# MLP products of two x tiles ahead of the projections, and adds moved from VectorE to DMA

## Chip, cores and metric

The kernel runs on one core of a Trainium2 chip. The metric is device time in microseconds of one execution; lower is better. Engines are called as the profile calls them: PE (TensorE), PEld (its weight loads), DVE (VectorE), ACT (ScalarE), POOL (GpSimd) and SP (SyncE). SP, ACT and POOL each also issue DMA transfers on a queue of their own.

## What is computed

Two branches on one input x (2048 rows of 512, bf16) are mixed by a gate per row. Cut to what matters:

```python
g = sigmoid((x * gate_w).sum(-1))
# A: 32 heads of 16; each row attends to 8 rows, 2 apart, behind it
q, k, v = split(x @ wqkv)
logits = einsum("bhsd,bhswd->bhsw", q, k[pos - 2*w]) * 16 ** -0.5     # w = 0..7
attn = softmax(where(pos - 2*w >= 0, logits, -1e9))
a = einsum("bhsw,bhswd->bhsd", attn, v[pos - 2*w]) @ wo
# B: an MLP over the rows, after a layer norm over the 512 columns
u = gelu(einsum("bsd,sf->bdf", layernorm(x), w1) + b1)                # F = 1792
b = transpose(einsum("bdf,fs->bds", u, w2) + b2)
out = g * a + (1 - g) * b
```

The inputs A_x and B_x have the same shape; both branches of the kernel read A_x.

## The kernel before

The program records every operation of every engine in a list with its reads and writes. A planner (`_Sched`) gives each operation an expected duration, runs a list schedule over five engines and so writes out the order on each engine; `plan_waits` then turns what is left of the dependences into semaphore waits. Each engine executes its list strictly in order. PE's main operations (`PE(...)`) are chained in the order of the program; only a few, such as the head-dim sums, are placed by the planner among them. The lists are emitted inside an `nc.Block()`, one function per engine (L890 to L908).

**Projections.** x is needed transposed (XT). The first 512 rows are transposed on PE (L548) and copied out by DVE and ACT (`ext`, L559); the other three groups of 512 rows come by transposing DMAs on SP's queue (L476). `f_q0` (L569) computes the first 512 rows of Q in two halves with 256-column matmuls, and `f_proj` (L613) everything else: K, Q and V, each in four head-dim groups `dl` and four row groups `sb`, four matmuls of 512 columns each. ACT copies each result from its PSUM bank (line L443 is the helper of all ACT operations). The banks rotate over seven, for V over three.

**Layer norm.** DVE computes statistics of the 16 x tiles (L652), some tiny operations give mean and deviation of all tiles at once (ACT: Ln and Exp), and 16 operations (L666) normalise X in place.

**Attention.** DVE does the work (L440 is the helper of all its two-input operations). The rows are handled in two halves h. For each half: four products `qk` of a Q group with eight shifted views of a K group, 8192 elements per partition each (two halves of 4096 in h = 0), two adds `qa` that join pairs of them, into buffers P0 to P2. Then `f_sum` (L683) on PE sums over the head-dim that lies across partitions, with a 0/1 matrix, reading both of the remaining buffers and accumulating them in PSUM banks 4 to 7; in h = 0 it also computes the gate's dot products (L677). ACT copies the logits out (`lev`), DVE and ACT do the softmax (`mx`, `msub`, `exp`, `sm`, `lns`, `rsz`, `rb`, `nrm`), and 16 DMAs per half on POOL's queue (L735) spread the weights over partitions. Then come the weighted values in eight units of 256 rows: a product `avm` of 8192 elements per partition, and adds of 4096 (`ava`), 2048 (`avb`) and 1024 (`avc`), the last into OT. Even units use buffer P1 and odd ones P0.

**MLP.** `f_ph2` (L769): 14 tiles of F, each 16 matmuls over the x tiles, W1 in three rotating slots, GELU on ACT. `f_ph3` (L795): 16 output tiles of rows, each 14 matmuls (the last tile in two column halves), with W2 in slots that reuse the memory of finished tensors. The attention's output product `f_wo` (L804, 4 matmuls) adds into the same bank, five tiles behind the MLP product; ACT scales and shifts the result by the gate (`ev`) and SP stores it. Unit u of the attention serves output tiles 2u and 2u + 1, so the last tiles wait for the last sum of unit 7.

Of the kernel before, what the change touches and what calls it, by code (L numbers as in the profile page):

```python
# [12 lines left out]
S = 2048  # L13
D = 512
# [13 lines left out]
NOELIDE = False  # L28

# [40 lines left out]
class _Sched:  # L70
# [72 lines left out]
    def _pass(self, ops, extra, dma_bw, dma_lat):  # L143
# [20 lines left out]
        dma_free = 0.0  # L164
# [8 lines left out]
        while nleft:  # L173
# [21 lines left out]
            if op.is_dma:  # L195
                clock[e] = st + op.dur
                xs = max(st + 0.3, dma_free)
                xd = max(op.nbytes / dma_bw, 0.05)
                dma_free = xs + xd
                op.end = max(dma_free, clock[e]) + dma_lat  # L200
            else:
                op.end = st + op.dur
                clock[e] = op.end
# [98 lines left out]
def bass_gated_mix__sliding_local_dilated__mixer_token_mlp__prompt_kernel(nc, A_x, A_wqkv, A_wo, B_x, B_w1, B_b1, B_w2, B_b2, gate_w, out, dbg=None):  # L302
    with contextlib.ExitStack() as es:
        block = es.enter_context(nc.Block())
# [56 lines left out]
        XTALL = ["xt0_%d_%d" % (hb, d0) for hb in range(2) for d0 in (0, 2)] + ["xt1", "xt2", "xt3"]  # L361
# [5 lines left out]
        PR = [["p0"], ["p1"], ["p2", "p2h"]]  # L367
# [4 lines left out]
        PB = [view("P%d" % b, BF16, [(HS, NW), (1, HS)]) for b in range(3)]  # L372
# [45 lines left out]
        NMR = small(NST)  # L418
        E1 = small(NST)
# [77 lines left out]
        ld_wq("wq0", 0, 2, "wq0")  # L497
        ld_wq("wq1", 2, 4, "wq1")
        ld_x(0, 1)
        ld_x(1, 1)  # L500
        ld_x(2, 2)
        ld_w("wk", 1, 0, 4, "wk")
        ld_xt(1)
# [10 lines left out]
        def ld_w1(j):  # L514
            load("w1_%d" % j, W1W[:, j % 3, :, :], w1v[:, :, 256 * j:256 * j + 256], S * 256 * 2, ["w1s%d" % (j % 3)], order=j < 3)
# [10 lines left out]
        def f_warm(n):  # L526
            def fn(e):
                ins = None
                for _ in range(n):
                    ins = e.matmul(ps[:, 7, :], lhsT=ONES, rhs=ONES4, start=True, stop=True)  # L530
                return ins
            return fn
# [8 lines left out]
        PE(f_warm(5), 2.1, ["ones"], ["b7"], "warm")  # L541

        def f_tx(t):
            def fn(e):
                ins = None
                for dt in range(4):
                    o_ = (dt % 2) * 256 + (t % 2) * 128
                    ins = e.transpose(out=psb(4 + 2 * (t // 2) + dt // 2)[:, o_:o_ + 128],  # L548
                                      in_=X[:, t, dt * 128:(dt + 1) * 128], identity=IDENT)
                return ins  # L550
            return fn

        def xt_ev(hb):
            for eng, d0 in (("dve", 0), ("act", 2)):
                bk = 4 + 2 * hb + d0 // 2
                src = psb(bk)[:, 0:512]
                dst = sub(XT, d0 * S + hb * 256, [(S, 2), (1, 256)])
                if eng == "dve":
                    A("dve", (lambda s_, d_: lambda e: e.tensor_copy(out=d_, in_=s_))(src, dst), 0.4, reads=["b%d" % bk],  # L559
                      writes=["xt0_%d_%d" % (hb, d0)], name="ext%d_%d" % (hb, d0))  # L560
                else:
                    A("act", act(dst, src, AF.Copy), 0.6, reads=["b%d" % bk],
                      writes=["xt0_%d_%d" % (hb, d0)], name="ext%d_%d" % (hb, d0))

        def f_q0(hb, dt):
            def fn(e):
                ins = None
                for dl in range(4):
                    ins = e.matmul(ps[:, dl, hb * 256:hb * 256 + 256], lhsT=sub(WQKV, dt * 3 * D + dl, [(4, 128)]),  # L569
                                   rhs=XT[:, dt, hb * 256:hb * 256 + 256], start=(dt == 0), stop=(dt == 3))  # L570
                return ins
            return fn

        for hb in range(2):
            for t in (2 * hb, 2 * hb + 1):
                PE(f_tx(t), 0.35, ["x%d" % t, "ident"], ["b%d" % (4 + 2 * hb), "b%d" % (5 + 2 * hb)], "tx%d" % t)
            xt_ev(hb)
            for dt in range(4):
                PE(f_q0(hb, dt), 0.44, ["xt0_%d_%d" % (hb, 2 * (dt // 2)), "wq%d" % (dt // 2)], ["b%d" % dl for dl in range(4)], "q0_%d_%d" % (hb, dt))
        XT0 = ["xt0_%d_%d" % (hb, d0) for hb in range(2) for d0 in (0, 2)]  # L580
# [18 lines left out]
        for dl in range(4):  # L599
            evac(0, dl, 0, dl)  # L600

        ring = [0, [4, 5, 6, 7, 0, 1, 2]]
# [15 lines left out]
        WR = {0: ["wq0", "wq1"], 1: ["wk"], 2: ["wv"]}  # L618
# [6 lines left out]
        def f_tb(e):  # L625
            e.transpose(out=psb(3)[:, 0:NFT], in_=B1R, identity=IDENT[0:NFT, 0:NFT])
            e.transpose(out=psb(3)[:, 64:68], in_=GWR, identity=IDENT[0:4, 0:4])
            return e.transpose(out=psb(3)[:, 32:32 + NST], in_=B2R, identity=IDENT[0:NST, 0:NST])

        for dl in range(4):  # L630
            proj(1, dl, 0)
        PE(f_tb, 0.3, ["b1r", "b2r", "gwr", "ident"], ["b3"], "t_b12")
        A("dve", lambda e: e.tensor_copy(out=GWREP, in_=sub(psb(3), 64, [(1, 4), (0, 32)])), 0.2, reads=["b3"], writes=["gwrep"], name="gwrep", prio=-20)
        A("dve", lambda e: e.tensor_copy(out=B1C, in_=psb(3)[:, 0:NFT]), 0.15, reads=["b3"], writes=["b1c"], name="b1c", prio=-20)
        A("dve", lambda e: e.tensor_copy(out=B2C, in_=psb(3)[:, 32:32 + NST]), 0.15, reads=["b3"], writes=["b2c"], name="b2c", prio=-20)
        for dl in range(4):
            proj(0, dl, 1)
            proj(1, dl, 1)
# [6 lines left out]
        ring[0], ring[1] = 0, [0, 1, 2]  # L645
        for dl in range(4):
            for sb in range(4):
                proj(2, dl, sb)


        for t in range(NST):
            A("dve", (lambda t_: lambda e: e.bn_stats(out=ST6[:, t_, :], in_=X[:, t_, :]))(t), 0.67,  # L652
              reads=["x%d" % t], writes=["st%d" % t], name="st%d" % t, prio=-20)
        STS = ["st%d" % t for t in range(NST)]
# [3 lines left out]
        A("dve", tt(MD, MD, MD, ALU.mult), 0.12, reads=[], writes=["md"], name="ln_md2", prio=-20)  # L658
        A("dve", lambda e: e.scalar_tensor_tensor(out=VV, in0=MD, scalar=128.0, in1=VV, op0=ALU.mult, op1=ALU.add), 0.12,
          reads=["md"], writes=["vv"], name="ln_var", prio=-20)  # L660
        A("act", act(SD, VV, AF.Ln, bias=1e-5, scale=1.0 / 512), 0.25, reads=["vv"], writes=["sd"], name="ln_log", prio=-20)
        A("act", act(RSTD, SD, AF.Exp, scale=-0.5), 0.25, reads=["sd"], writes=["rstd"], name="ln_rstd", prio=-20)
        A("dve", lambda e: e.scalar_tensor_tensor(out=NMR, in0=MS, scalar=-0.5, in1=RSTD, op0=ALU.mult, op1=ALU.mult), 0.15,
          reads=["ms", "rstd"], writes=["nmr"], name="ln_nmr", prio=-20)
        for t in range(NST):
            A("dve", (lambda t_: lambda e: e.tensor_scalar(out=X[:, t_, :], in0=X[:, t_, :], scalar1=col(RSTD, t_), scalar2=col(NMR, t_),  # L666
                                                           op0=ALU.mult, op1=ALU.add))(t), 0.33,
              reads=["rstd", "nmr", "st%d" % t], writes=["x%d" % t], name="ln%d" % t, prio=-10)


        def f_sum(h, b0, b1, with_gate):
            def fn(e):
                ins = None
                if with_gate:
                    for dt in range(4):
                        for c in range(4):
                            ins = e.matmul(ps[32 * c:32 * c + 32, 3, :], lhsT=GWREP[:, dt, :],  # L677
                                           rhs=sub(XT, dt * S + c * UT_, [(HS, 2), (1, UT_)]),
                                           start=(dt == 0), stop=(dt == 3), tile_position=(0, 32 * c))
                for wp in range(4):  # L680
                    for k_, b_ in enumerate((b0, b1)):
                        for c in range(4):
                            ins = e.matmul(ps[32 * c:32 * c + 32, 4 + wp, :], lhsT=RP,  # L683
                                           rhs=sub(PB[b_], 2 * wp * HS + c * UT_, [(HS, 2), (1, UT_)]),
                                           start=(k_ == 0), stop=(k_ == 1), tile_position=(0, 32 * c))
# [4 lines left out]
        PLAN = {0: ((0, 1), (1, 2)), 1: ((2, 0), (0, 1))}  # L690
        for h in range(2):
            for pr in range(2):
                bb = PLAN[h][pr]
                for k_ in range(2):
                    dl = 2 * pr + k_
                    for s_, n_ in (((0, 512), (512, 512)) if h == 0 else ((0, HS),)):
                        sbs = [2 * h + x_ for x_ in range(s_ // 512, (s_ + n_) // 512)]
                        A("dve", tt(sub(PB[bb[k_]], s_, [(HS, NW), (1, n_)]), sub(QH[h], dl * HS + s_, [(0, NW), (1, n_)]),
# [238 lines left out]
```

## Time and profile before

| | |
|---|---|
| time, median of 3 runs | 172.63 us (171.09 to 173.3) |
| profiled execution, first to last instruction (its span) | 170.8 us |
| around the span (172.63 less 170.83) | 1.8 us, if the profiled execution was like the median one |
| PE busy | 164.1 us |
| DVE busy | 152.3 us, of which 134.7 in L440 |
| ACT busy | 79.4 us |
| POOL busy | 19.5 us, 16.3 of it issuing the 32 DMAs of L735 |
| last sum on DVE ends | 166.2 us |
| PE ends | 168.2 us |

The page of the profile gives the busy time of each engine, the chain of work that ended last (followed backwards from the last instruction to what released it), and groups of instructions with their busy time, mean time of one, and idle time ahead. Further answers of the trace give the instructions in order of time. Lines of the form "start, us, engine line op xcount [idle before <- who ended it]" are such an answer; matmuls overlap in the pipeline, so a group's total is divided by its count, and the mean of a single one is longer than the distance to the next.

### The profile page before, as it was taken

The numbers are of one execution on the slowest core, as the hardware profiler recorded it, in microseconds if no ns is written. First come the engines' busy times: TensorE is split into PE (matmuls) and PEld (weight loads), VectorE is DVE, ScalarE is ACT, GpSimd is POOL, SyncE is SP. The second block draws the span as 40 slices with busy tenths as digits, with TensorE's granted clock in tenths as the row PEclk, the third lists the DMA queues.
The fourth block names the chain that finished last, engine by engine and source line by source line (L and its number), as shares of the span: only waits on it lengthen the run. The fifth ranks groups of instructions, "written<-read, shape, count | busy, mean of one in ns | idle before, by whom it ended". The sixth has DMA issues, their size and how long they took to land.

```text
span 170.8 us, 2097 instructions
## 1 busy us (share of the span) xinstructions
PE 164.1 (96%) x846; PEld 79.8 (47%) x846; DVE 152.3 (89%) x115; ACT 79.4 (46%) x107; POOL 19.5 (11%) x57
## 2 busy tenths in 40 slices
PE   6889999999999999999999998999999999999983
PEld 2574555555554444444443443444444444444732
DVE  2516998999999989999998998999999999999981
ACT  3119677666665189987424697000022211111172
POOL 7000000000000000000198001970000000000000
PEclk9999999999999999999999999999999999999999
DMA  5999999800000095987599999998000010100023
GB/s 165 273 240 267 300 300 290 256 1 2 4 0 0 26 308 135 285 210 209 160 240 230 360 301 283 308 351 285 7 31 31 31 35 31 60 32 31 31 74 110
DMA packets 43128, 26.87 MB, mean 157 GB/s; under 512 B 7536, under 2 KB 41968, under 8 KB 43120
## 3 DMA queue, kind: packets, MB, share of 16 engines
q1 hardware_dynamic: 40800, 21.96, 47.9%
q0 software_dynamic: 1632, 4.21, 7.9%
q10 hardware_dynamic: 688, 0.59, 1.1%
q8 instruction: 6, 0.10, 0.2%
q14 instruction: 2, 0.02, 0.0%
HBM read 18.88 MB, written 2.10 MB: 123 GB/s over the span
## 4 chain that ended last, share of the span: by engine, by line
DVE 51%; PE 33%; ACT 6%; DMA 4%; issue 3%; POOL 1%; SPq 0%; DVEq 0%
DVE arena L440 50%; PE ps L613 22%; PE ps L769 4%; ACT arena L443 4%; PE ps L569 3%; ACT L872 2%; DMA arena<-arena 2%; DMA arena<-in_A_x_dram 2%; PE ps L804 1%; PE ps L683 1%; POOL arena L735 1%; PE ps L677 1%; PE ps L548 1%; DVE arena L559 0%; DVE arena L652 0%
## 5 line engine op out<-in xcount | busy, mean ns | idle before, releaser
L440 DVE TENSOR_TENSOR arena<-arena 128x2048 bf16<-128x2048 bf16 (+10 forms) x72 | 134.7, 1902 | 3.5 <-PE ps L683 1.0
L795 PE MATMUL ps<-arena 128*128 128x512 bf16 (+1 forms) x238 | 50.3, 367 | 0.7 <-ACT arena L443 0.7
L443 ACT ACTIVATE arena<-ps,arena 128x512 bf16<-128x512 f32 (+1 forms) x30 | 21.5, 727 | 60.9 <-PE ps L804 49.8
L769 PE MATMUL ps<-arena 128*128 128x512 bf16 x224 | 49.0, 379 | 0.0
L443 ACT ACTIVATE arena<-ps 128x512 bf16<-128x512 f32 (+3 forms) x53 | 33.4, 649 | 23.7 <-PE ps L613 10.4
L613 PE MATMUL ps<-arena 128*128 128x512 bf16 x176 | 38.3, 379 | 0.0
L795 PEld LDWEIGHTS ps<-arena 128*128 128x128 bf16 x238 | 23.2, 98 | 26.2 <-ACT arena L443 1.2
L769 PEld LDWEIGHTS ps<-arena 128*128 128x128 bf16 x224 | 21.7, 98 | 26.6 <-issue 0.8
L613 PEld LDWEIGHTS ps<-arena 128*128 128x128 bf16 x176 | 19.8, 113 | 17.7
L735 POOL DMA_DIRECT2D arena<-arena x32 | 16.3, 515 | 93.8 <-DVE arena L440 93.8
L872 ACT ACT_TABLE_LOAD x14 | 18.0, 1283 | 2.1 <-issue 1.8
L804 PE MATMUL ps<-arena 128*128 128x512 bf16 (+1 forms) x68 | 15.8, 367 | 0.7 <-DVE arena L440 0.7
L652 DVE BATCH_NORM_STATS2 arena<-arena 128x6 f32<-128x512 bf16 x16 | 10.1, 681 | 4.3 <-DMA arena<-in_A_x_dram 4.3
L804 PEld LDWEIGHTS ps<-arena 128*128 128x128 bf16 x68 | 6.6, 98 | 8.1 <-DVE arena L440 1.2
L443 ACT ACTIVATE arena<-arena 128x16 f32<-128x16 f32 (+5 forms) x10 | 6.8, 679 | 2.5 <-DVE arena L440 2.4
L569 PE MATMUL ps<-arena 128*128 128x256 bf16 x32 | 5.5, 346 | 1.0 <-DVE arena L559 1.0
L666 DVE TENSOR_SCALAR arena<-arena 128x512 bf16<-128x512 bf16 x16 | 5.3, 405 | 0.0
L569 PEld LDWEIGHTS ps<-arena 128*128 128x128 bf16 x32 | 3.9, 129 | 2.5 <-DVE arena L559 1.6
L683 PE MATMUL ps<-arena 128*32 128x512 bf16 x64 | 3.8, 380 | 0.0
L559 DVE COPY arena<-ps 128x512 bf16<-128x512 bf16 x2 | 0.8, 425 | 3.0 <-PE ps L548 3.0
L530 PE MATMUL ps<-arena 128*128 128x512 bf16 x5 | 2.3, 629 | 1.1 <-POOL arena L446 1.1
L548 PE MATMUL ps<-arena 128*128 128x128 bf16 x16 | 2.3, 308 | 0.6 <-DMA arena<-in_A_x_dram 0.6
(34 smaller groups left out, 13.0 us busy)
## 6 DMA issues: line engine op xcount, KB each, us to landing
arena<-in_B_w_dram SPq DMA_DIRECT2D x7, 1024.0 KB, 8.1
arena<-in_B_w_dram SPq DMA_DIRECT2D x8, 896.0 KB, 8.6
arena<-arena POOLq DMA_DIRECT2D x32, 128.0 KB, 7.3
out_dram<-arena SPq DMA_DIRECT2D x15, 128.0 KB, 1.7
arena<-in_A_x_dram SPq DMA_DIRECT2D x3, 512.0 KB, 4.3
arena<-in_A_wqkv_dram SPq DMA_DIRECT2D x2, 512.0 KB, 6.0
arena<-in_A_wqkv_dram ACTq DMA_DIRECT2D x2, 256.0 KB, 3.6
arena<-in_A_wo_dram SPq DMA_DIRECT2D x1, 512.0 KB, 8.7
```

The costliest lines, as they stand in the source:

```text
L440: return lambda e: e.tensor_tensor(out=o_, in0=a_, in1=b_, op=op_)
L443: return lambda e: e.activation(out=o_, in_=i_, func=f_, **kw)
L569: ins = e.matmul(ps[:, dl, hb * 256:hb * 256 + 256], lhsT=sub(WQKV, dt * 3 * D + dl, [(4, 128)]), rhs=XT[:, dt, hb * 256:hb * 256 + 256], ...
L613: ins = e.matmul(ps[:, bank, :], lhsT=sub(WQKV, dt * 3 * D + tn * D + dl, [(4, 128)]), rhs=XT[:, dt, sb * 512:(sb + 1) * 512], start=(dt = ...
L652: A("dve", (lambda t_: lambda e: e.bn_stats(out=ST6[:, t_, :], in_=X[:, t_, :]))(t), 0.67, reads=["x%d" % t], writes=["st%d" % t], name="s ...
L666: A("dve", (lambda t_: lambda e: e.tensor_scalar(out=X[:, t_, :], in0=X[:, t_, :], scalar1=col(RSTD, t_), scalar2=col(NMR, t_), op0=ALU.mu ...
L683: ins = e.matmul(ps[32 * c:32 * c + 32, 4 + wp, :], lhsT=RP, rhs=sub(PB[b_], 2 * wp * HS + c * UT_, [(HS, 2), (1, UT_)]), start=(k_ == 0), ...
L735: prev = sch.dma("pool", (lambda d_, s_: lambda e: e.dma_start(d_, s_))(dst, src), 131072, ds, issue=1.0, reads=["att%d" % h], writes=["av ...
L769: ins = e.matmul(ps[:, bank, :], lhsT=W1W[:, (ft // 2) % 3, st, 128 * (ft % 2):128 * (ft % 2) + 128], rhs=X[:, st, :], start=(st == 0), st ...
L795: ins = e.matmul(ps[:, bank, 0:c1 - c0], lhsT=W2S[i // 2][:, ft, 128 * (i % 2):128 * (i % 2) + 128], rhs=UT[:, ft, c0:c1], start=(ft == 0) ...
L804: ins = e.matmul(ps[:, bank, 0:c1 - c0], lhsT=OT[:, i // 2, dl, 128 * (i % 2):128 * (i % 2) + 128], rhs=WO[:, dl, c0:c1], start=False, sto ...
L872: e.preload_act_table_set(want)
```

## The change

- **Lead.** Two x tiles are normalised alone and at once: their own statistics, aggregate (`bn_aggr`), Ln, Exp and scaling. `f_lead` then does the matmuls of these tiles for the first GL = 4 tiles of F, into banks 0 to 3, before any projection. The partial sums stay there until the MLP's own time, when these four F tiles begin at x tile 2. The parts of W1 that this needs (`ld_strip`) come on ACT's queue at the start; the loads of W1 slots 0 and 1 leave them out. Around the transposes stand 8 filler matmuls on constants instead of 5.
- **Start.** x tiles 2 and 3 are loaded separately; Wq is loaded whole on SP's queue after Wk, no longer in two parts on ACT's. The 256-column Q matmuls are gone: all 48 projections are of the same form, in the order K, K, Q, Q first. Projections rotate over banks 4 to 7 only, MLP tiles over 0 to 3.
- **Gate.** Its products stand after the Q and K projections, its transposes between the V projections, instead of beside and after the first head-dim sum.
- **Head-dim sums.** `f_sum` reads one buffer. In h = 0 the four products go to P0, P1, P2 and a fourth buffer laid over LOG and ATT; P1 is added to P0 by a DMA on POOL's queue (`qd0`, accumulating), the other two adds are on DVE. In h = 1 all three adds are on DVE.
- **Weighted values.** For units 1 to 6 the 4096-wide add is an accumulating DMA (`avd`) on POOL's queue, 1 MB each. Units 0 and 7 keep theirs on DVE.
- **End of the MLP.** The first three output tiles are done as three first halves, then three second halves.
- **Block.** The engines' lists are emitted directly, without `nc.Block()`.
- **Planner.** It now keeps POOL's transfers apart from the others when it counts DMA time.

```diff
+NLEAD = 2
+AVD = (1, 2, 3, 4, 5, 6)
+GL = 4
...
-        block = es.enter_context(nc.Block())
...
+        def ld_strip(t):
+            load("s%d" % t, W1W[:, 0:2, t, :], w1v[:, t, 0:512].rearrange("p (j c) -> p j c", j=2), 131072, ["w1a%d_%d" % (t, j) for j in range(2)], queue="act", order=False)
+
         ld_x(0, 1)
+        ld_strip(0)
         ld_x(1, 1)
-        ld_x(2, 2)
+        ld_strip(1)
+        ld_x(2, 1)
+        ld_x(3, 1)
         ld_w("wk", 1, 0, 4, "wk")
+        ld_w("wq", 0, 0, 4, "wq")
         ld_xt(1)
...
+        def f_lead(t):
+            def fn(e):
+                ins = None
+                for ft in range(GL):
+                    ins = f_ph2(ft, ft, t, t + 1)(e)
+                return ins
+            return fn
+
+        PE(f_warm(6, 7), 2.5, [], ["b7"], "warm0")
+        tx(0)
+        PE(f_warm(1, 7), 0.43, [], ["b7"], "warm1")
+        tx(1)
+        PE(f_warm(1, 7), 0.43, [], ["b7"], "warm2")
...
+            PE(f_lead(t), 0.87, ["x%d" % t, "w1a%d_0" % t, "w1a%d_1" % t], ["b%d" % ft for ft in range(GL)], "lead%d" % t)
+            if t == 0:
+                tx(2)
+                tx(3)
...
-        ring = [0, [4, 5, 6, 7, 0, 1, 2]]
+        ring = [0, [4, 5, 6, 7]]
...
+        for tn, dl in ((1, 0), (1, 1), (0, 0), (0, 1), (1, 2), (0, 2), (1, 3), (0, 3)):
+            proj(tn, dl, 0)
...
             if h == 0:
...
+                qk(0, 0)
+                qk(1, 1)
+                rows = [(2048, 4), (1, 2048)]
+                sch.dma("pool", (lambda d_, s_: lambda e: e.dma_start(d_, s_, accum_op=ALU.add, max_dma_last_dim=4096))(sub(PB[0], 0, rows), sub(PB[1], 0, rows)),
+                        int(3.2e6), sch.dsem("qd%d" % h), issue=1.0, reads=PR[1], writes=PR[0], name="qd%d" % h)
+                qk(2, 2)
+                qk(3, 3)
+                qadd(2, 3)
+                qadd(2, 0)
+                fin = 2
+            else:
+                qk(0, 0)
+                for dl in range(1, 4):
+                    qk(dl, 1)
+                    qadd(0, 1)
+                fin = 0
...
-            A("dve", tt(pv[:, 0:4], pv[:, 0:4], pv[:, 4:8], ALU.add), 2.28, writes=["p%d" % b], name="ava%d" % u)
...
+            if u in AVD:
+                sch.dma("pool", (lambda d_, s_: lambda e: e.dma_start(d_, s_, accum_op=ALU.add, max_dma_last_dim=4096))(
+                    sub(PB[b], 0, [(2048, 2), (1, 2048)]), sub(PB[b], 4096, [(2048, 2), (1, 2048)])),
+                    int(1.6e6), sch.dsem("avd%d" % u), issue=1.0, writes=["p%d" % b], name="avd%d" % u)
+            else:
+                A("dve", tt(pv[:, 0:4], pv[:, 0:4], pv[:, 4:8], ALU.add), 2.28, writes=["p%d" % b], name="ava%d" % u)
...
+        for half in range(2):
+            for i in range(3):
+                ph3(i, half)
+        for i in range(3, L):
+            ph3(i, 0)
+            ph3(i, 1)
...
-        @block.sync
-        def _(e):
-            emit_engine("sp", e)
...
+        emit_engine("sp", nc.sync)
+        emit_engine("act", nc.scalar)
+        emit_engine("pool", nc.gpsimd)
+        emit_engine("dve", nc.vector)
+        emit_engine("pe", nc.tensor)
```

The order that the planner then writes for DVE near the end is: avm1, ..., avm2, avb1, avc1, avm3, avb2, avc2, avm4 and so on to avm7, ava7, avb6, avc6, avb7, avc7: each unit's second add stands behind the next unit's product. On POOL's queue the 16 DMAs of the second half stand in three groups between the accumulating ones: 7 after avd1, 4 after avd2, 5 after avd3.

## The prediction

> **What bounds the kernel now.** I read the busy table first, then the chain that ended last, then the waits, then the start and the end of PE in order of time.
>
> Busy time and chain, from the page:
>
> ```profile
> span 170.8 us, 2097 instructions
> ...
> PE 164.1 (96%) x846; PEld 79.8 (47%) x846; DVE 152.3 (89%) x115; ACT 79.4 (46%) x107; POOL 19.5 (11%) x57
> ...
> DVE 51%; PE 33%; ACT 6%; DMA 4%; issue 3%; POOL 1%; SPq 0%; DVEq 0%
> ```
>
> PE is busy for 96%, yet half of the chain is DVE: the two run side by side and finish together, so time goes only where PE gets less to do or waits less, and only while DVE doesn't become the later one. PE in order of time at the start:
>
> ```profile
> 1.07 2.32 PE L530 MATMUL ps<-arena 128*128 128x512 bf16 x5 [1.07 <-POOL arena L446]
> 3.57 0.59 PE L548 MATMUL ps<-arena 128*128 128x128 bf16 x4 [0.19 <-DMA arena<-in_A_x_dram]
> 4.60 0.61 PE L548 MATMUL ps<-arena 128*128 128x128 bf16 x4 [0.44 <-DMA arena<-in_A_x_dram]
> 5.73 3.60 PE L569 MATMUL ps<-arena 128*128 128x256 bf16 x16 [0.52 <-DVE arena L559]
> 9.13 1.06 PE L548 MATMUL ps<-arena 128*128 128x128 bf16 x8
> 10.71 1.94 PE L569 MATMUL ps<-arena 128*128 128x256 bf16 x16 [0.52 <-DVE arena L559]
> ```
>
> Sixteen equal matmuls take 3.60 us at 5.73 and 1.94 at 10.71: PE is at half pace until about 10 us (the granted-clock row reads full throughout and doesn't show it). From 12.6 on PE has two gaps, one before each of these:
>
> ```profile
> 106.44 16.79 PE L795 MATMUL ps<-arena 128*128 128x512 bf16 x77 [0.69 <-ACT arena L443]
> ...
> 166.25 1.91 PE L804 MATMUL ps<-arena 128*128 128x512 bf16 x12 [0.68 <-DVE arena L440]
> ```
>
> The second says that the last DVE sum (ended 166.21) is late for the last output product, by less than 1 us.
>
> **Prices.** From the chain in order of time (start, us, what) and from the groups by shape (busy us and mean ns after the bar):
>
> ```profile
> 16.26 34.66 PE ps L613 x160
> ...
> 58.80 1.76 PE ps L683 x32
> ```
> ```profile
> L440 DVE TENSOR_TENSOR arena<-arena 128x8192 bf16<-128x8192 bf16 x16 | 70.7, 4419 | 1.7 <-PE ps L683 1.0 <-DMA arena<-arena 0.6
> ...
> L440 DVE TENSOR_TENSOR arena<-arena 128x4096 bf16<-128x4096 bf16 x16 | 36.3, 2287 | 0.3
> ...
> L440 DVE TENSOR_TENSOR arena<-arena 128x2048 bf16<-128x2048 bf16 x12 | 14.7, 1223 | 0.3
> ```
>
> **PE, term by term.** One 512-column matmul in a row of them costs 34.66 / 160 = 0.2166 us.
>
> *Start.* Before, the first 16 matmuls' worth of projection is inside 5.73 to 12.64. Now all 192 projection matmuls come after the lead, which does 8 of the 224 MLP matmuls. The same finish would need projections to start at T0 = 12.64 + (8 - 16) x 0.2166 = 10.9. I work T0 out: x tile 0 is there at 3.46 (DVE's first statistics, before). Statistics 0.69, aggregate 0.17 (a 16-column DVE row), Ln and Exp 0.21 each (128x16 on ACT) with ACT's 0.60 copy of the first transpose ahead of them, then 0.41 for the normalising: the first lead matmul at 5.65. Lead 4 x 0.43, transposes 0.9, second lead 1.7 at half pace: 9.95. At full pace the three are 0.87, 0.5, 0.87: 7.9. WK is no later: before, it landed 5.9 after its issue at 2.20, so 8.1, with 0.25 MB more ahead of it on the two queues than now. Half pace on until 10.7 costs another 0.4. So T0 is between 7.9 and 10.4; PE now has matmuls or transposes in nearly all of 0.8 to 9, where it had holes of 0.44 and 0.52, so I take **9.4**: 1.5 gained.
>
> The Trainium skill ("TensorE: Matmul & The Clock Gate", Part 1) gives about 3.4 us of sustained activity until the clock opens, in windows that run freely. By that rule PE would be fast from 4.2 to 7.6, T0 about 8.3 and the time about 1 us lower than mine; the row above, still slow at 9 after a first matmul at 1.07, is the reason that I don't follow it.
>
> *Sums.* L683 falls from 64 to 32 matmuls; 32 took 1.76: 1.76 gained, over both halves. The price is one 8192-wide DVE add more (4.42), below.
>
> *Ladder.* T0 9.4; 32 projections 27.7, small transposes 0.16, gate 0.98 (as before, moved), 4 V projections 3.46, gate transposes 0.3, 12 V projections 10.4: 52.4. Fourteen MLP matmuls 3.0, head sum 0 0.88: 56.3. 162 more 35.1: 91.4. Head sum 1 0.88, 40 more 8.7. From the first L795 to PE's end it was 104.08 to 168.18 = 64.1; the two gaps (0.69, 0.68) leave 62.7: the new order of first and second halves lets PE start on halves whose GELU is long done, which answers the first gap.
>
> **DVE, beside it.** The first product starts at T0 + 3.5 = 12.9 (third and first projection, a 0.60 copy); it was 16.66. Then by row: halves 2.28, stats 0.617, copies 0.45, small ones 0.7, normalising 0.329, full products and adds 4.43.
> - Four halves, 12 stats, the copies (a half waits for a projection copied at about 20.8): 30.0. Small ones, one half, 14 normalisings, three halves: 44.4. Gate 0.6: 45.0; PE's pjv1_3 needs this bank at 44.7, a stall of 0.3 at most.
> - Two adds: 53.9, where PE reaches head sum 0 at 55.4. One more add of this half went to the DMA qd0: issued at 23.8, needed at 49.5, 25.7 us for 2.1 MB.
> - Two products 62.8, softmax 65.7, add 70.1, sums 72.5, product, 0.42, add 81.8, normalise 83.0, product and add **91.9**. PE is at head sum 1 by 91.4: a stall of **0.5**. Each us that DVE is later here is a us of PE.
>
> PE's end: 91.9 + 0.9 + 8.7 + 62.7 = 164.2. From PE's end to the span's end stays 2.62 (168.18 to 170.80): span 166.8. Around the span stays 1.8 (172.63 less 170.83, taking the profiled run for a median one; the three runs lie 1.3% apart). Without the block each engine has a branch less at both ends; 0 to 0.3, I take 0.1. Time: **168.5**, 2.4% below the median.
>
> **The DMA adds, which have no row.** Six adds of 2.28 (13.7 us) leave DVE; units 1 to 6 now wait for a POOL-issued transfer of 1.05 MB between SBUF and SBUF. Let D be the time from the product's end to the landing. Low end: plain copies. The shortest of L735 took 3.0 us for 128 KB, 2.7 without its bytes. In 116 to 124 us POOL's queue (packets, MB, share of 16 engines) is nearly alone:
>
> ```profile
> q0 software_dynamic: 336, 0.89, 31.2%
> q1 hardware_dynamic: 202, 0.10, 4.2%
> ```
>
> 31.2% of 8 us for 0.89 MB is 2.9 us for 1.05 MB: D = 5.6. High end: the only transfer in this trace that works on data is the transposing one, 0.5 MB in 5.4 to 7.3, so 10.8 to 14.6. An add reads two and writes one in the same 4 KB pieces as the copies; I take twice the copy, **D = 8.6**.
>
> Between a product's end and its second add lie two short adds and the next product, 6.4 us; the wait repeats at every other unit. DVE: product 0 ends at 96.3, max and subtract 99.1, product 1 103.5, sums, first add, normalise, last add 111.8, product 2 116.2, unit 1 done 118.2, product 3 122.6. From there the last sum ends at 3.9 + the later of 137.7 + 2D and 129 + 3D: **158.8** at D = 8.6, 154.3 at 5.6 (there nothing waits). PE wants it at 164.2 - 1.9 = 162.3, so it is hidden up to **D = 9.8**; beyond that each us of D costs 3 us. On POOL the 16 copies of the second half stand behind adds 2 and 3 and so behind products 2 and 3; the last is issued by about 126 and product 7 wants it at 146. If POOL's issue grows with rows (516 ns at 32 rows, 527 at 14 to 16: no growth seen), that is part of D. Should the first add (12.7 us of time) meet the W2 loads, it still fits.
>
> The Trainium skill ("SBUF — State Buffer", Summary: rules for kernel authors) advises against hiding a POOL-issued DMA under DVE work, since descriptor writing can be locked out. Here the 32 issues of L735 took 508 to 535 ns while DVE ran its adds, so not under these; under the 14 normalisings (2-port, by that page) no row shows it. If qd0 were held until 37.6 and took twice a copy, it would land at 52.0, and the sum would be 2.5 us higher.
>
> **Rivals.**
> 1. *The adds are slow* (the other side). Mechanism: DVE waits for avd2, avd4 and avd6 until its last sum comes after PE's need. Decides from D = 9.8; equal to before at 11.2, 2% slower at 12.3. At 14.6: last sum 176.7, time 182.9. For it: the transposing row. Against it: long pieces, idle queues after 119 us. Chance of being slower by 2%: 0.12; of D between 9.8 and 12.3 (168.5 to 176): 0.10.
> 2. *The start gives nothing, DVE sets the pace in the middle.* Loads come a us later (strips on ACT's queue; x3 and WQ put the first transposing load 0.9 later on SP), half pace lasts, T0 is 10.9, and the extra add makes head sum 1 wait 1.5 rather than 0.5: 168.5 + 1.5 + 1.0 = 171.0. With four banks for projections instead of seven, an ACT hiccup reaches PE sooner (0.60 of ACT per 0.87 of PE leaves 0.27): part of this case. Chance 0.20.
> 3. *The change does what it says* but with a quick clock: T0 8.3, time 167.4; inside the first case.
>
> **How the numbers follow.** The forecast case (PE bound, adds hidden) has 0.58 and reaches from 166.5 (T0 at 7.9 to 8, no stall) to 170.3 (T0 10.4, a us of stall); about four fifths of it lie under 169.2, the 2% line, which with three runs 171.09 to 173.3 is about what can be told from no change. So faster 0.50 (with a little from rival 1's edge), same 0.38, slower 0.12. The range: 166.4 to 173.6, which leaves out most of the slow adds.
>
> **What would show it.** T0: first projection at 8.5 to 10. PE without gaps until head sum 1, 0 to 1 us there, none before the first MLP output product. Waits of DVE for DMA of 2 us or so before each of avb2 and avb4. PE's end about 164, last DVE sum 3 us or more ahead of its products. It is wrong if D is over 10, if DVE reaches head sum 1 late by over 2 us, or if half pace reaches into the projections.

## The result, and the profile after

The changed kernel takes 166.25 us (median of 4 runs, 165.56 to 167.46) beside 171.94 for the kernel before on the same chip. The ratio is 0.970, 95% interval 0.962 to 0.978: 3.0% faster. (Medians and ranges here are of all runs; the ratios leave out runs over 1.5% above the fastest of the same kernel and are not exactly the quotient of two medians, which is 0.967 here.) The forecast was 168.5 us, 2.4% under the earlier median, in a range of 166.4 to 173.6; its faster side had 0.50. The measured 166.25 lies just under the low end of that range; the ratio of 0.970, taken of the earlier median of 172.63, would be 167.4, inside it.

The profiled execution took 165.56 us with a span of 164.3. Its busy table and its chain, from the page:

```profile
span 164.3 us, 2007 instructions
...
PE 160.6 (98%) x801; PEld 76.5 (47%) x801; DVE 142.7 (87%) x111; ACT 77.7 (47%) x109; POOL 28.5 (17%) x64
...
PE 97%; DVE 1%; ACT 1%; issue 0%
```

Before, the chain was half DVE; now it is PE from the first matmul to the last, with one wait of 0.62 us, ahead of the first lead. PE lost 3.5 us of busy time, and DVE 9.6 although one large add was added to it. The spans of the two profiled executions differ by 6.5 us: about 3 of it is the start (the projections begin at 7.85, where 10.9 would finish as before), 1.8 the shorter head-dim sums, 1.4 the two gaps and 0.4 the end behind PE.

PE in order of time at the start (start, us, operation, idle before it and who ended it):

```profile
0.85 2.72 PE L545 MATMUL ps<-const-bfloat16-1.0 128*128 128x512 bf16 x6 [0.85 <-PEq L962]
...
4.26 0.41 PE L560 MATMUL ps<-arena 128*128 128x128 bf16 x4
4.50 0.38 PE L545 MATMUL ps<-const-bfloat16-1.0 128*128 128x512 bf16 x1
5.50 1.04 PE L578 MATMUL ps<-arena 128*128 128x512 bf16 x4 [0.62 <-DVE arena L604]
6.38 0.61 PE L560 MATMUL ps<-arena 128*128 128x128 bf16 x8
6.92 1.04 PE L578 MATMUL ps<-arena 128*128 128x512 bf16 x4
7.85 8.82 PE L641 MATMUL ps<-arena 128*128 128x512 bf16 x40
```

The last filler takes 0.38, the single one before it 0.61: PE is at full pace from about 4.5 us, where it was at half pace until 10. The two leads cost 0.88 and 0.93 from their start to the next start, and the projections start at 7.85; the forecast had 9.4. From there to PE's end at 162.1 the rows show no gap, so the four banks of the projections were enough. The forecast wait of 0.5 at the second head-dim sum isn't there: DVE's last add for it ends at 88.7, and PE gets there at 90.09.

DVE near its end, in order of time:

```profile
123.03 6.41 DVE L445 TENSOR_TENSOR arena<-arena 128x2048 bf16<-128x2048 bf16 x3 [4.02 <-DMA arena<-arena]
131.59 6.41 DVE L445 TENSOR_TENSOR arena<-arena 128x2048 bf16<-128x2048 bf16 x3 [2.16 <-DMA arena<-arena]
139.84 6.41 DVE L445 TENSOR_TENSOR arena<-arena 128x2048 bf16<-128x2048 bf16 x3 [1.84 <-DMA arena<-arena]
146.51 12.46 DVE L445 TENSOR_TENSOR arena<-arena 128x2048 bf16<-128x2048 bf16 x8 [0.26 <-DMA arena<-arena]
```

These are the waits for the adds in the DMA: 4.02, 2.16, 1.84 and 0.26 us, 8.3 in all, in front of avb2, avb3, avb4 and avb5: at four units in a row, where the forecast had them at every other one (avb2, avb4), each shorter than the one before. The last sum ends at 146.51 + 12.46 = 158.97. PE's last row is

```profile
156.72 5.35 PE L851 MATMUL ps<-arena 128*128 128x512 bf16 x28
```

and it wants the last sum for the last 12 of these, 1.9 us before its end, at 160.2. So 1.2 us are to spare.

### The profile page after: what moved, and what is told of

Its sections match the earlier page's. It is cut to its first block, busy times and chain, and to the rows that moved or that the text cites. A ratio compares the mean times of both kernels' runs of the same rounds, so it can differ in the third digit from the quotient of the medians.

```text
span 164.3 us, 2007 instructions
## 1 busy us (share of the span) xinstructions
PE 160.6 (98%) x801; PEld 76.5 (47%) x801; DVE 142.7 (87%) x111; ACT 77.7 (47%) x109; POOL 28.5 (17%) x64
## 4 chain that ended last, share of the span: by engine, by line
PE 97%; DVE 1%; ACT 1%; issue 0%
PE ps L578 30%; PE ps L842 29%; PE ps L641 25%; PE ps L851 8%; PE ps L545 2%; PE ps L734 1%; PE ps L665 1%; PE ps L560 1%; ACT arena L448 1%; DVE arena L897 0%; DVE arena L604 0%; PE ps L701 0%; PE ps L655 0%; PE ps L657 0%; PE ps L656 0%
## 5 line engine op out<-in xcount | busy, mean ns | idle before, releaser
L445 DVE TENSOR_TENSOR arena<-arena 128x8192 bf16<-128x8192 bf16 (+9 forms) x67 | 125.6, 1906 | 13.1 <-DMA arena<-arena 8.3
L578 PE MATMUL ps<-arena 128*128 128x512 bf16 x224 | 49.2, 379 | 0.6 <-DVE arena L604 0.6
L448 ACT ACTIVATE arena<-ps 128x512 bf16<-128x512 f32 (+3 forms) x54 | 34.8, 644 | 18.1 <-PE ps L641 13.5
L641 PE MATMUL ps<-arena 128*128 128x512 bf16 x192 | 42.2, 379 | 0.0
L842 PEld LDWEIGHTS ps<-arena 128*128 128x128 bf16 x238 | 23.3, 98 | 25.3
L578 PEld LDWEIGHTS ps<-arena 128*128 128x128 bf16 x224 | 21.6, 98 | 27.4 <-DVE arena L604 1.0
L641 PEld LDWEIGHTS ps<-arena 128*128 128x128 bf16 x192 | 21.4, 113 | 19.7 <-ACT arena L448 0.4
L796 POOL DMA_DIRECT2D arena<-arena x32 | 17.5, 694 | 62.9 <-DVE arena L445 62.9
L810 POOL DMA_DIRECT2D arena<-arena x6 | 7.3, 1224 | 37.4 <-DVE arena L445 37.4
L851 PEld LDWEIGHTS ps<-arena 128*128 128x128 bf16 x68 | 6.7, 98 | 7.2
L448 ACT ACTIVATE arena<-arena 128x1 f32<-128x1 f32 (+6 forms) x14 | 7.6, 542 | 1.6 <-DVE arena L445 1.3
L724 DVE TENSOR_SCALAR arena<-arena 128x512 bf16<-128x512 bf16 x14 | 4.6, 412 | 0.0
L545 PE MATMUL ps<-const-bfloat16-1.0 128*128 128x512 bf16 x8 | 3.7, 593 | 0.8 <-PEq L962 0.8
L756 POOL DMA_DIRECT2D arena<-arena x1 | 1.4, 1381 | 18.1 <-DVE arena L445 18.1
L897 DVE TENSOR_SCALAR arena<-ps,arena 128x256 bf16<-128x256 f32 x1 | 0.5, 543 | 3.1 <-PE ps L851 3.1
L734 PE MATMUL ps<-arena 128*32 128x512 bf16 x32 | 2.1, 382 | 0.0
(37 smaller groups left out, 14.8 us busy)
```

Of the source, the lines that this page charges most:

```text
L445: return lambda e: e.tensor_tensor(out=o_, in0=a_, in1=b_, op=op_)
L448: return lambda e: e.activation(out=o_, in_=i_, func=f_, **kw)
L545: ins = e.matmul(ps[:, bank, :], lhsT=WONE, rhs=WROW, start=True, stop=True)
L578: ins = e.matmul(ps[:, bank, :], lhsT=W1W[:, (ft // 2) % 3, st, 128 * (ft % 2):128 * (ft % 2) + 128], rhs=X[:, st, :], start=(st == 0), st ...
L641: ins = e.matmul(ps[:, bank, :], lhsT=sub(WQKV, dt * 3 * D + tn * D + dl, [(4, 128)]), rhs=XT[:, dt, sb * 512:(sb + 1) * 512], start=(dt = ...
L796: prev = sch.dma("pool", (lambda d_, s_: lambda e: e.dma_start(d_, s_))(dst, src), 131072, ds, issue=1.0, reads=["att%d" % h], writes=["av ...
```

## The experiments

All are compared with the kernel before on the same chip, whose medians lay between 171.9 and 172.6 us; they ran on several chips, so the ratios compare variants more safely than the medians. The ratio of the changed kernel itself is 0.970 (0.962 to 0.978). Not taken back singly were the new order and form of the projections, the gate's place and the order of the loads.

### The six adds back on DVE

```diff
-AVD = (1, 2, 3, 4, 5, 6)
+AVD = ()
```

> The changed kernel with the 4096-wide adds of units 1 to 6 back on DVE (no avd). Theory 'the DMA adds keep DVE away from the end': DVE loses 8.3 us of waits for DMA and gets 6 x 2.28 = 13.7 us of adds, so the last sum moves from 158.97 to about 164.4 while the last output products want it at 160.2: PE waits about 4 us there, time about 170.4 (166.25 + 4.2). Rival 'PE alone bounds it, the six adds were free on DVE': time 166.2 and no gap before the last products.

Measured: 174.72 us, ratio 1.019 (1.009 to 1.030). The DMA adds are needed, and more than the theory said. PE at the end of this kernel, and the granted clock in four stretches of the end (busy us of each engine, then granted clock, DMA share, GB/s):

```profile
156.70 1.89 PE L851 MATMUL ps<-arena 128*128 128x512 bf16 x8
164.99 5.19 PE L851 MATMUL ps<-arena 128*128 128x512 bf16 x20 [6.40 <-DVE arena L445]
```
```profile
150.00:158.00 8.00, 8.00 (x53) 4.96 (x52) 7.96 (x3) 1.75 (x3) 0.00 (x0) 1.00 0.09 33
...
161.00:168.00 7.00, 3.01 (x8) 1.09 (x9) 5.72 (x5) 0.78 (x1) 0.00 (x0) 0.52 0.00 0
168.00:172.40 4.40, 2.18 (x14) 1.18 (x12) 0.54 (x1) 2.01 (x3) 0.00 (x0) 0.98 0.36 119
```

PE stands for 6.40 us, where 4.2 was expected (the last sum of DVE ends at 166.8, not 164.4: the planner put DVE's work in another order, with 4 us more of waiting for ACT). The clock falls while PE stands: finer stretches of this trace read 1.00 up to 161.2, 2.6 us into the wait, and 0.50 from 161.4 to 168.0. So the last 20 products take 5.19 us, 1.4 more than at full pace (3.77, next experiment). 6.40, 1.4 and 0.3 at the seam between the two rows make the 8.1 us by which this span (172.4) is longer. The planner's other order has a part in the 6.40, so this is the price of the six adds together with it.

### The same with PE kept busy in its wait

```diff
 AVD = ()
...
         for i in range(L - LAG, L):
+            if i == 12:
+                PE(f_warm(30, banks[9]), 0.01, [], ["b%d" % banks[9]], "warm_end")
             finish_tile(i)
```

> The kernel with the six adds back on DVE (no avd) and 30 filler matmuls on constants ahead of the products of units 6 and 7, so that PE is busy for 6.5 us in place of its wait of 6.4. Theory 'a wait of several us lowers PE's pace for what follows': the last 20 products take 3.5 us instead of 5.19, time about 1.7 us under the same kernel without the fillers (174.72), 173.0. Rival 'the long last products are only their waits': 174.7 or a little more.

Measured: 173.06 us, ratio 1.007 (1.003 to 1.011). PE and the granted clock at the end:

```profile
158.92 6.73 PE L545 MATMUL ps<-const-bfloat16-1.0 128*128 128x512 bf16 x30
165.49 3.77 PE L851 MATMUL ps<-arena 128*128 128x512 bf16 x20
```
```profile
161.00:168.00 7.00, 7.00 (x33) 2.90 (x31) 6.22 (x6) 1.35 (x2) 0.00 (x0) 1.00 0.02 7
```

The products after the fillers take 3.77 instead of 5.19, the clock is granted in full, and the median is 1.7 us lower. The intervals of the two ratios just overlap; the clock settles it, since its mean over the whole execution is 0.97 to 0.98 in all four runs without the fillers and 1.00 in all ten with them. A wait of PE of this length costs its length and then a slow stretch, and the slow stretch can be bought off with work that has no use.

### The add of the first half back on DVE

```diff
-                rows = [(2048, 4), (1, 2048)]
-                sch.dma("pool", ... accum_op=ALU.add ... name="qd%d" % h)
+                qadd(0, 1)
```

> The changed kernel with the DMA add of the first half (qd0) back on DVE: one 8192-wide add more, 4.43 us. The planner puts the head-dim sums later among PE's MLP matmuls. Theory 'DVE has 1 to 3 us to spare at each meeting point': last DVE sum at about 163.4 against a need at 160.2, time about 166.25 + 3.2 = 169.4; less if the later place of the first sum lets DVE's waits for the weight transfers shrink, not under 167.5. Rival 'DVE had room for the add': time 166.2.

Measured: 174.11 us, ratio 1.007 (1.002 to 1.012). The miss has the same shape as in the first experiment. PE at the end:

```profile
157.38 1.89 PE L849 MATMUL ps<-arena 128*128 128x512 bf16 x8
164.54 6.45 PE L849 MATMUL ps<-arena 128*128 128x512 bf16 x20 [5.26 <-DVE arena L445]
```

DVE's last sum ends at 166.3 instead of 158.97: 4.4 of it is the add, 2.2 more is waiting for DMA (10.5 us instead of 8.3) and 0.9 waiting for ACT. PE waits 5.26, and the rest takes 6.45 where 3.77 is full pace. One add of 4.4 us on DVE costs 6.4 us by the ratios and 7.9 by the medians: the change's whole gain, so both sets of DMA adds are needed together.

### The six transfers as copies, without adding

```diff
-                sch.dma("pool", (lambda d_, s_: lambda e: e.dma_start(d_, s_, accum_op=ALU.add, max_dma_last_dim=4096))(
+                sch.dma("pool", (lambda d_, s_: lambda e: e.dma_start(d_, s_, max_dma_last_dim=4096))(
```

> The changed kernel with the six avd transfers as plain copies of the same bytes and pieces: the add of the upper half of the weighted values is left out there, so the attention part of the output is another. Theory 'an add in the DMA costs about twice a copy, and all of it is hidden': issue to landing falls from 7.8 to 12.3 (median 10.0) to about 5.5 to 6.5, DVE's waits for DMA (8.3 us) go, its last sum ends near 151, and the time stays at 166.2. Rival 'the adds' length shows in the time': time about 165.

Measured: 165.85 us, ratio 0.964 (0.956 to 0.971), which doesn't differ from the changed kernel's. For the six transfers the profiles say, as copies:

```profile
L810 POOL DMA_DIRECT2D arena<-arena x6: 706/714/724, 100.9 to 138.7; - x6
...
DMA to landing us min/median/max: 4.5/5.6/8.4
```

and as adds, in the changed kernel:

```profile
L810 POOL DMA_DIRECT2D arena<-arena x6: 1194/1232/1239, 100.5 to 146.5; - x6
...
DMA to landing us min/median/max: 7.8/10.0/12.3
```

An add takes 1.8 times the time of a copy from issue to landing (medians of 10.0 and 5.6), and 0.5 us more of POOL to issue (1.23 against 0.71). DVE's waits for DMA go, its last sum ends at 150.7, 8 us earlier, and the time doesn't follow: the adds' length is hidden as forecast.

### The adds in pieces of 1 KB

```diff
-                    sub(PB[b], 0, [(2048, 2), (1, 2048)]), sub(PB[b], 4096, [(2048, 2), (1, 2048)])),
+                    sub(PB[b], 0, [(512, 8), (1, 512)]), sub(PB[b], 4096, [(512, 8), (1, 512)])),
```

The limit on the piece's length was set to 1024 with it.

> The changed kernel with the six avd adds in pieces of 1 KB instead of 4 KB, the same bytes. Theory 'the end hangs on D, the time from a product's end to its add's landing, with 1.2 us to spare': POOL's issue grows with the pieces (0.51 us for 32, 1.23 for 256, so about 3.7 for 1024), the transfer by about a sixth, D by 3.3 us; DVE waits at three units, its last sum comes 8 to 10 us later, PE stands 7 to 9 us before the last products and then works at half pace: time 175 to 178. Rival 'the piece doesn't matter': time 166.2.

Measured: 165.99 us, ratio 0.966 (0.960 to 0.972). A miss: the piece didn't matter for the time. POOL's issue grew to 1.59 us, not to 3.7; issue to landing was 8.3 to 14.8 with a median of 9.7 (7.8 to 12.3 and 10.0 with 4 KB); DVE waited 9.0 us instead of 8.3. The experiment was meant to lengthen D by three us and didn't, so what one us of D costs was measured only from the other side, by the copies.

### The lead taken back

```diff
-            PE(f_lead(t), 0.87, ["x%d" % t, "w1a%d_0" % t, "w1a%d_1" % t], ["b%d" % ft for ft in range(GL)], "lead%d" % t)
...
-            s0 = NLEAD if ft < GL else 0
+            s0 = 0
```

> The changed kernel with the eight lead matmuls back in the MLP's own time (the two tiles are still normalised early, the W1 strips still loaded first). Theory 'the lead fills a time in which PE has nothing else': projections start at about 7.6 instead of 7.85, 8 x 0.2166 = 1.7 us of matmuls come back later, so about +1.5 us, time 167.7. Rival 'the lead matters for the clock': with PE idle from 5 to 7.6 it stays at half pace until about 10.4, the first projections cost 1.3 us more, time about 169. Rival 'no gain from the lead, the start is set by loads': time 166.2.

Measured: 169.73 us (167.39 to 171.44 in ten runs), ratio 0.982 (0.975 to 0.988). The profiled execution (171.39) is one of the longest of the ten, so its rows show what makes the long ones:

```profile
6.00 0.62 PE L560 MATMUL ps<-arena 128*128 128x128 bf16 x8 [1.12 <-DMA arena<-in_A_x_dram]
9.57 11.17 PE L640 MATMUL ps<-arena 128*128 128x512 bf16 x40 [2.95 <-DMA arena<-in_A_wqkv_dram]
```
```profile
7.60:14.40 6.80, 4.83 (x12) 1.76 (x13) 0.39 (x2) 1.19 (x2) 0.00 (x0) 0.50 1.16 216
14.40:20.00 5.60, 5.60 (x28) 2.90 (x26) 4.63 (x3) 3.67 (x7) 0.00 (x0) 1.00 1.06 234
```

Two gaps of 1.12 and 2.95 us follow each other, and from 7.6, 1 us into the second, to 14.4 the clock is granted at half. Of the 5.8 us by which this span is longer, 1.7 is the later start of the projections, 2.4 the half pace (11.17 instead of 8.82 for the first 40 matmuls) and 1.7 the eight matmuls that come later. This is near the rival's effect, but not its mechanism: PE doesn't stay at half pace, it reaches full pace (four transposes in 0.39 at 4.27) and loses it again. The mean granted clock of the ten runs is 0.98 in the two longest, 0.99 in five and 1.00 in three, the two shortest among these; the shortest are near the theory's 167.7. The gap's releaser is new: the load of WK lands at 9.5, 6.9 us after its issue at 2.67, where it was there by 7.84 in the changed kernel. In the variant with head-dim sums over two buffers, below, WK comes as late (9.38), but the lead is in its place, the gap is 1.56, and the 22 matmuls behind it take 4.91 us, which is full pace. So in these two traces the lead keeps the clock up when the load is late.

### No fillers

```diff
-        PE(f_warm(6, 7), 2.5, [], ["b7"], "warm0")
...
-        PE(f_warm(1, 7), 0.43, [], ["b7"], "warm1")
...
-        PE(f_warm(1, 7), 0.43, [], ["b7"], "warm2")
```

> The changed kernel without any of the eight filler matmuls. Theory 'early full pace comes from nearly gapless PE work from 0.85 on': without them lead, transposes and second lead run at half pace (1.7 + 0.9 + 1.7 us from 5.5), projections start at about 9.9 instead of 7.85 and the first ones may be slow, time about 168.3 to 168.8. Rival 'the pace rises at a fixed time after the start, whatever PE does': projections still start at about 7.9, time 166.2.

Measured: 167.67 us, ratio 0.976 (0.969 to 0.984); medians 1.4 us over the changed kernel's, with intervals that overlap. The start on PE:

```profile
5.47 1.89 PE L578 MATMUL ps<-arena 128*128 128x512 bf16 x4 [0.75 <-DVE arena L601]
7.15 1.06 PE L560 MATMUL ps<-arena 128*128 128x128 bf16 x8
8.01 1.91 PE L578 MATMUL ps<-arena 128*128 128x512 bf16 x4
9.71 6.66 PE L638 MATMUL ps<-arena 128*128 128x512 bf16 x27
```

The leads take 1.89 and 1.91 instead of 1.04, and the projections start at 9.71 (9.9 expected), the first of them still slow (27 in 6.66 us); the span is 2.5 us longer. Full pace is earned by early work on PE; it doesn't come at a fixed time.

### The kernel before, with the changed kernel's fillers

```diff
-        PE(f_warm(5), 2.1, ["ones"], ["b7"], "warm")
+        PE(f_warm(6), 2.5, [], ["b3"], "warm0")
...
             for t in (2 * hb, 2 * hb + 1):
                 PE(f_tx(t), 0.35, ...)
+                if hb == 0:
+                    PE(f_warm(1), 0.43, [], ["b3"], "warm%d" % (t + 1))
```

> The kernel before with the changed kernel's fillers alone: six matmuls on constants first, one more after each of the first two tile transposes. Theory 'half of the gain at the start is pace': the first 16 projection matmuls of 256 columns take about 1.95 us instead of 3.60 at 5.7, everything behind moves by 1.5 to 1.7 us, time about 170.3 against 171.9. Rival 'the gain at the start is only the order of the work': time as before, 171.9, and still 3.6 us for the first half.

Measured: 171.11 us, ratio 0.995 (0.991 to 0.999). The first half of the Q projection in 256-column matmuls:

```profile
6.20 1.94 PE L572 MATMUL ps<-arena 128*128 128x256 bf16 x16 [0.44 <-DVE arena L562]
...
10.88 3.62 PE L618 MATMUL ps<-arena 128*128 128x512 bf16 x16
```

1.94 us instead of 3.60, as expected; the first L618 is at 10.88 instead of 12.48, and the profiled span is 169.4, 1.4 us less. The timed gain is only 0.5% with an interval of 0.1 to 0.9%, so the size expected in time (0.9%) is at its edge. The runs of the kernel before on this chip may say why: six lie at 170.7 to 171.1 us and eleven at 172.4 to 173.0, while all ten with the fillers lie at 170.8 to 171.8. It fits a half pace that without the fillers ends early in some runs; but only one run of the kernel before has a trace, so this isn't shown.

### Head-dim sums over two buffers again

```diff
-                qadd(2, 0)
-                fin = 2
+                fin = (2, 0)
...
-                for dl in range(1, 4):
+                for dl in range(1, 3):
                     qk(dl, 1)
                     qadd(0, 1)
-                fin = 0
+                qk(3, 2)
+                fin = (0, 2)
```

`f_sum` accumulates the two buffers in PSUM as in the kernel before.

> The changed kernel with both head-dim sums over two buffers, as before, and so one 8192-wide DVE add less in each half. Theory 'PE bounds from the first matmul to the last': 32 matmuls of 0.061 come back, +1.9 us on PE, DVE is 8.9 us lighter and its last sum 5 us or more earlier, time 166.25 + 1.9 = 168.1. Rival 'DVE bounds through its last sum': time falls, 165 or less.

Measured: 168.56 us, ratio 0.978 (0.971 to 0.985). DVE's busy time is 133.8 us, 8.9 less, and the span is longer: PE is the bound, and behind its gap for WK it waits for nothing. (The intervals of the two ratios touch.) One part was a miss: DVE's last sum came at 159.2, not 5 us earlier, since DVE waited 12.6 us for DMA instead of 8.3. The size fits the 1.9 us expected only in part, since in the profiled execution WK lands late:

```profile
6.80 1.03 PE L578 MATMUL ps<-arena 128*128 128x512 bf16 x4
9.38 4.91 PE L641 MATMUL ps<-arena 128*128 128x512 bf16 x22 [1.56 <-DMA arena<-in_A_wqkv_dram]
```

Its span of 167.8 is 3.5 us over the changed kernel's: 1.56 is this gap, 1.9 the sums.

### The old order of the first output tiles

```diff
-        for half in range(2):
-            for i in range(3):
+        for i in range(3):
+            for half in range(2):
                 ph3(i, half)
```

> The changed kernel with the first three output tiles of the MLP in the old order (both halves of a tile, then the next). Theory 'the new order answers the gap of 0.69 us before the second output tile': a gap of 0.5 to 2 us appears there, since the last GELU now ends at 102.4 and the second half of the first tile would start at 101.2: time 0.7 to 1.5 us more, about 167. Rival 'the GELU is early enough by itself': time 166.2, no gap.

Measured: 167.28 us, ratio 0.975 (0.968 to 0.981). The gap is back, 1.04 us in front of the second half of the first tile:

```profile
102.33 16.79 PE L842 MATMUL ps<-arena 128*128 128x512 bf16 x75 [1.04 <-ACT arena L448]
```

The intervals of the two kernels overlap, so the time alone doesn't show it (the medians are 1.0 us apart); the gap does.

### ACT's Ln and Exp of the leading tiles first

```diff
-            A("act", act(col(RSTD, t), col(SD, t), AF.Exp, scale=-0.5), ... name="rs%d" % t, prio=-40)
+            rs_ = A("act", act(col(RSTD, t), col(SD, t), AF.Exp, scale=-0.5), ... name="rs%d" % t, prio=-40)
+            ext(t, after=[rs_])
```

> The changed kernel with ACT's Ln and Exp of the two leading tiles ahead of its copies of their transposes. Theory 'the start is set by the chain of the first tile': the first lead matmul starts at 5.1 instead of 5.5, PE idles 0.2 instead of 0.6 us, projections start up to 0.4 us earlier, time 165.8 to 166.2. Rival 'the start is set by the arrival of x tiles 2 and 3 and of WK': projections start at 7.85 or later as before, time 166.2.

Measured: 166.29 us in six runs, ratio 0.966 (0.960 to 0.972): no difference from the changed kernel. In its profiled execution:

```profile
5.27 1.04 PE L582 MATMUL ps<-arena 128*128 128x512 bf16 x4
...
8.59 3.62 PE L646 MATMUL ps<-arena 128*128 128x512 bf16 x16 [0.65 <-DMA arena<-in_A_wqkv_dram]
```

The lead starts 0.23 earlier, and then PE stands before the projections for WK. The rival holds: the load ends this start. None of the variants is faster than the changed kernel clear of the noise.

### The block back

```diff
+        block = es.enter_context(nc.Block())
...
-        emit_engine("sp", nc.sync)
+        @block.sync
+        def _(e):
+            emit_engine("sp", e)
...
```

> The changed kernel with its lists emitted inside the block again. Theory 'the block costs a branch at both ends of each engine': 0.1 to 0.5 us, time 166.3 to 166.8, span as without it within 0.3. Rival 'the block explains the part of the gain that lies outside the span (172.63 - 170.83 = 1.8 before, 1.25 after)': time about 166.9 at an equal span.

Measured: 166.74 us, ratio 0.969 (0.960 to 0.978). The time doesn't tell it from the changed kernel. What lies around the span does, since time and span of every run are on record: 1.7 to 1.8 us in all four runs here, 1.2 to 1.3 in the four of the changed kernel, 1.2 to 1.6 in all other variants without the block. So some 0.5 us of the gain is the block's. The kernel before and its variant with fillers have 2.0 to 2.2 in every run, so 0.85 us of the gain lies outside the span; what the rest of it, 0.3 to 0.4, comes from is open.

## Why the prediction was right, and where it was off

The forecast case held: PE is the bound, the adds are hidden, faster by over 2%. Term by term:

- *T0.* Forecast 9.4, measured 7.85 in the profiled execution: the largest error of the sum. The step that was mis-sized is the pace: I charged half pace to nearly all of the leads and transposes (9.95 would be all), and PE was at full pace from about 4.5. The page "TensorE: Matmul & The Clock Gate" of the Trainium skill (Part 1, some 3.4 us of sustained activity) was the better guide; I set it aside for a row of the kernel before. What I missed in that row: there PE stood three times in its first 6 us (from 3.4, 4.2 and 5.2), while with the new fillers it works without a gap from 0.85 to 4.4. These fillers alone brought 1.94 for 3.60 in the kernel before, and without any the leads took 1.89.
- *WK and the spread of T0.* "No later than 8.1" held in the changed kernel's profile (by 7.84) and failed in others (8.6, 9.4, 9.5, all issued at 2.67). The pace has a spread too: in three variants with the same start (the add of the first half on DVE, the copies, the block) the first lead was still partly slow, 1.42 to 1.55 instead of 1.04, and the projections started at 8.2 to 8.3. So T0 is 7.7 to 8.3 by the pace, and only the load carried it to the forecast's 9.4.
- *Sums.* 1.76 forecast; undoing it lengthened the span by 3.5, of which 1.6 is the late WK and 1.9 the sums.
- *The gaps.* Both went, 0.69 and 0.68. The order of halves answers the first: with the old order it returns as 1.04.
- *Head sum 1.* A stall of 0.5 was forecast, none came. DVE started 1.6 us earlier (11.29 for 12.9), through T0, and had gained 3.2 by there (88.7 for 91.9).
- *D.* Forecast 8.6, measured 7.8 to 12.3 from issue to landing with a median of 10.0; from the product's end it is 0.3 more. The low end, a plain copy at 5.6, was met by the copies' median. The step that was mis-sized is the add: I doubled only the 2.9 us of the transfer, so that 8.6 is 1.5 times a copy; measured it is 1.8 times. In order the six adds took 11.2, 10.0, 12.3, 10.1, 8.2 and 7.8; the first three are those between which the 16 copies stand on POOL's queue, so part of the excess may be these copies, which no run separates. "Wrong if D is over 10" was met at its edge.
- *DVE's end.* DVE waited for the adds 8.3 us in all where the forecast had 4.5 (158.8 less 154.3). The last sum still ended at 158.97 against a forecast of 158.8, because DVE came to these adds 3.6 us earlier than forecast (product 3 ends at 119.0, forecast 122.6): two errors that cancelled, which is luck. PE's need also came earlier, at 160.2 instead of 162.3; with both shifts the forecast's own rule hides the adds up to 10.3 instead of 9.8, so there was next to nothing to spare by it, and 1.2 us were left where over 3 had been expected.
- *Rival 1* priced a late DVE at 3 us per us of D. No run lengthened the median of D, so the price isn't tested; from adds to copies, 4.4 us of D less, the last sum came 8.2 earlier, 1.9 per us. It leaves out what follows once PE has to wait: the kernels with the six adds, and with the first half's add, back on DVE show products slowed by 1.4 (5.19 less 3.77) and 2.7 us (6.45 less 3.77) on top of the waits.
- *Rival 2* didn't come: T0 was 7.85 and not 10.9, and PE had no gap in the projections or at head sum 1. Its first condition did hold: the first transposing load was issued at 3.70 instead of 2.72.
- *Around the span.* 1.8 was carried over, with 0.1 for the block. The 1.8 took a time and a span from different runs; within one run it is 2.0 to 2.2 before, and 1.24 was measured after, 0.5 of the difference through the block.

Adding up: PE's end 164.2 against 162.1 is T0 (1.55) and the stall (0.5). The span's end comes 2.2 after it instead of 2.62, and 1.24 around it instead of 1.7. That leads from 168.5 to 165.6, the profiled execution; the median is 0.7 above it, with spans of 164.3 to 166.2.

The other passage on a page of the skill, "SBUF — State Buffer" (Summary: rules for kernel authors), is that the descriptors of a POOL-issued transfer are held up while DVE works in its double or fourfold mode. The case that I feared didn't come up: qd0's issue ran from 22.1 for 1.38 us, while DVE ran statistics and 7 us before its normalisings, and it landed 18.0 us after its start, at 40.1, with the add that reads it starting at 47.0. No run here issues a transfer under the normalisings.

## What to carry to other kernels

Where one engine is busy to 96% and another nearly so, work moved from the second to DMA pays only by what it saves the first from waiting; here the rest of the gain hung on it, since one add of 4.4 us put back on DVE costs 6 to 8. Price a wait of PE of several us as its length plus a stretch at half pace behind it (1.4 to 2.7 us more here behind waits of 6.40 and 5.26; a wait of 1.56 had none), and fill the start: early work without gaps, even useless work, was worth 1 to 2 us. Ask of a load that must land at a fixed point how much it varies, not only when it landed in one execution.

## What the runs showed that I had not expected

- The granted clock fell to half while PE stood, and not at a fixed time in its wait: 2.6 to 2.8 us into the wait of 6.40, 4.1 to 4.3 into the one of 5.26, and in the kernel without the lead 1 us into a gap that followed another of 1.12. In all three traces it stayed there for some 6.8 us (161.3 to 168.2, 163.4 to 170.3, 7.6 to 14.4), though PE came back to work at 165.0, 164.5 and 9.6.
- The granted-clock row reads 1.00 in the first microseconds even where matmuls run at half pace (the kernel before, 3.60 for 16); the matmuls' own durations show it.
- A 0.5 MB load issued at the same 2.67 us landed by 7.74 in one variant and at 9.5 in another. Loading WK ahead of x tiles 2 and 3 might give it room; no run has it.
- Pieces of 1 KB and of 4 KB made little difference to an accumulating DMA of 1 MB (median 9.7 and 10.0 us, longest 14.8 and 12.3).
- The spare time at the end is small: 1.2 us in the changed kernel, and in the variant with Ln and Exp first PE already waited 0.5 us there for DVE.
